# Attention then SwiGLU on one core: PSUM shared out anew, some transposes moved from TensorE to DMA, and the last stores halved

## The chip, the cores and the metric

The kernel runs on one core of a Trainium2 chip. The metric is the device time in microseconds, lower is better. Each kernel was run several times, but for one that got a single look; all runs quoted are of the fast state, but for that one, whose state is unknown. The profile is that of one such run (472.68 us for the kernel before, a run apart from those whose times are listed). "Span" is the time of the profiled execution on the core, about 2 us less than the device time of the same run (470.8 against 472.68 us).

The profile shows five engines: TensorE (PE in the profile, its weight loads PEld), VectorE (DVE), ScalarE (ACT), GpSimd (POOL) and the issuing SyncE (SP). What each waited for is what the profile infers from semaphore events. The kernel puts the results of matmuls in PSUM. A "bank" here is a buffer of up to 512 float32 a partition; the kernel's pools take eight, and in the trace VectorE and ScalarE empty them (a sum's two VectorE instructions take 177 and 424 ns, ScalarE's copy of an output product 491 ns). "Sums" are the products attn @ v of one head, "FFN" is the part after the RMS norm, and a "turn" is a transpose of a whole tile.

## The reference, cut to what matters

```python
# q, k, v: (8, 12, 448, 64)
scores = scale * q @ k^T;  m = max(scores);  e = exp(scores - m)
attn = e / (sum(e) + exp(-m) + 1e-9);  x = attn @ v          # -> (3584, 768)
xn = x / rms(x) * rms_g                                       # RMS norm
out = (silu(xn @ w_gate) * (xn @ w_val)) @ w_out              # 768 -> 1536 -> 768
```

## The kernel before

TensorE executes one hand-ordered stream. After the first batch, the FFN of batch b is woven with the attention of the batches after it: a list `ffn` of units (A: one gate or value product of six matmuls; B: one output product of twelve) gives the beat, and a list `ops` of everything else, each with a time in units, is popped when the beat reaches it. This fixes the *program order* on each engine.

In this kernel q, k and the normalised x have to be turned (transposed) before the matmuls that read them. Some are turned on TensorE into PSUM and copied out, the others by DMA:

```python
    NPE = 2          # batches whose x is turned on TensorE (0 and 1)
    NQPE = 7         # groups of four heads whose q, k are loaded as bf16; 0 to 6 are turned on TensorE
    ps_s = ...tile_pool(name="ps_s", bufs=2, space=PSUM)   # scores: 2 x 2 banks
    ps_u = ...tile_pool(name="ps_u", bufs=2, space=PSUM)   # sums (attn @ v), q/k turns, x turns
    ps_f = ...tile_pool(name="ps_f", bufs=2, space=PSUM)   # FFN products

    def emit_T(g):                                  # q/k turn of one head pair: 16 transposes, one copy
        ps = ps_u.tile([128, 2, C, P], BF16, name="qkt_ps", tag="u")
        ...                                         # nc.tensor.transpose x16
        nc.vector.tensor_copy(out=t[:, :, 0:S], in_=...)          # -> pair_t

    def emit_AV(g, hh):                             # sums of one head: 16 matmuls, emptied by VectorE
        u_ps = ps_u.tile([128, C, E1], FP32, name="u_ps", tag="u")
        ...
        nc.vector.reciprocal(out=recip, in_=u_ps[0:P, :, D:E1])
        nc.vector.tensor_tensor(out=x_tiles[b][...], in0=u_ps[...], in1=recip..., op=ALU.mult)

    def emit_turn_x(b, c):
        if b < NPE:
            ps = ps_u.tile([128, KD, P], BF16, name="xnt_ps", tag="u")
            ...                                     # 6 transposes, one copy
        else:
            nc.sync.dma_start_transpose(out=xnt[:, c, :, :], in_=xn[:, c, :])

    def load_w_o(i):                                # a third of w_out, float32 -> bf16, GpSimd's queue
        nc.gpsimd.dma_start(out=wo_bf[:, i * 4:(i + 1) * 4, :], in_=moe_w_out[i * 512:(i + 1) * 512, :]...)
    ...
    for i in range(KF // 4):
        ops.append((22.1 + 0.01 * i, lambda i=i: load_w_o(i)))
```

`g` counts pairs of heads (six to a batch, NP = 6). Line numbers such as L309 in the profiles are those of the kernel profiled: L309 in the kernel before and L312 in the changed one are the gate and value matmuls, L235 and L238 the sums.

The softmax here doesn't subtract the row's maximum and nothing guards it: scores larger than these inputs give would overflow.

## Time and profile before

475.25 us, median of the three runs (473.12 to 475.77).

From the profile's page, busy time by engine, and the span in 40 slices (busy tenths of TensorE, granted TensorE clock in tenths, busy share of the 16 DMA engines):

```profile
PE 456.7 (97%) x4048; PEld 246.7 (52%) x4048; DVE 241.1 (51%) x621; ACT 249.1 (53%) x365; POOL 95.8 (20%) x109
...
PE   7989998999999999999999989999999999999996
...
PEclk9999999999999999999999999999999999999999
DMA  8999974998099894693069796289015221100133
```

TensorE is the bound: busy 97% of the span, at full clock. What TensorE waited for, from the view of its waits (engine, line, what was waited for: us in total, times, longest):

```profile
PE v_ps L309 <- DVE ht_sb L320: 2.4, 6, 0.6
...
PE u_ps L235 <- DVE pair_t_102 L181: 0.6, 1, 0.6
```

The first is value products waiting for one of the two FFN banks.

### The profile page before, as it was taken

Reading aid. Unit: us, or ns where it says so; the run is one execution under the profiler, and the core shown is the slowest. Engines: PE = TensorE matmul, PEld = TensorE weight load, DVE = VectorE, ACT = ScalarE, POOL = GpSimd, SP = SyncE. Lnnn points to the kernel's source line nnn. Section 1 sums busy time; section 2 is a strip of 40 time slices with the busy share of each in tenths; the row PEclk is TensorE's granted clock in tenths of the full one; section 3 lists DMA queues with packets and bytes.
Section 4 is the critical chain, followed back from the end, with each engine's and each line's share of the span. In section 5 each row is a group of like instructions: output and inputs, shape, how many; then the busy total and the mean of one; then the engine's idle time right before and its main releaser. Section 6 shows DMA issues by size and latency. Waiting matters only on the chain.

```text
span 470.8 us, 9822 instructions
## 1 busy us (share of the span) xinstructions
PE 456.7 (97%) x4048; PEld 246.7 (52%) x4048; DVE 241.1 (51%) x621; ACT 249.1 (53%) x365; POOL 95.8 (20%) x109
## 2 busy tenths in 40 slices
PE   7989998999999999999999989999999999999996
PEld 3644544555555554544555544545455555555563
DVE  5676699455541276656532166755643247555200
ACT  4977764656555665545456555555556652222221
POOL 8424455123020222131011210313000000000000
PEclk9999999999999999999999999999999999999999
DMA  8999974998099894693069796289015221100133
GB/s 134 225 227 190 209 189 101 233 240 156 1 221 170 225 194 114 121 227 66 0 145 194 198 203 144 52 176 181 4 36 127 69 68 24 36 1 0 36 100 100
DMA packets 86776, 60.47 MB, mean 128 GB/s; under 512 B 50646, under 2 KB 81692, under 8 KB 86732
## 3 DMA queue, kind: packets, MB, share of 16 engines
q1 hardware_dynamic: 73820, 43.60, 42.5%
q0 software_dynamic: 12912, 16.26, 18.6%
q8 instruction: 31, 0.51, 0.5%
q14 instruction: 13, 0.11, 0.1%
HBM read 47.19 MB, written 11.01 MB: 124 GB/s over the span
## 4 chain that ended last, share of the span: by engine, by line
PE 85%; DVE 9%; ACT 4%; issue 1%; POOL 0%; DVEq 0%; ACTq 0%
PE o_ps L334 24%; PE v_ps L309 21%; PE g_ps L309 16%; PE u_ps L235 9%; PE s_ps L205 8%; PE s_ps L309 5%; DVE xsq L261 3%; DVE x_sb L239 1%; ACT p_sb_108 L210 1%; DVE ht_sb L320 1%; PE warm_ps L353 1%; ACT t_sb L313 1%; PE qkt_ps L178 1%; ACT p_sb_114 L210 1%; DVE x_sb L266 1%
## 5 line engine op out<-in xcount | busy, mean ns | idle before, releaser
L309 PE MATMUL v_ps<-xnt_sb,wv_bf 128*128 128x448 bf16 x576 | 125.0, 353 | 2.4 <-DVE ht_sb L320 2.4
L334 PE MATMUL o_ps<-wo_bf,ht_sb 128*128 128x384 bf16 x672 | 116.5, 326 | 0.0
L309 PE MATMUL g_ps<-xnt_sb,wg_bf 128*128 128x448 bf16 x444 | 96.4, 353 | 0.7 <-DVE silu_4291 L315 0.6
L334 PEld LDWEIGHTS <-ht_sb 128*128 128x128 bf16 x672 | 62.6, 98 | 46.2 <-issue 7.8
L309 PEld LDWEIGHTS <-wv_bf 128*128 128x128 bf16 x576 | 52.8, 97 | 54.5 <-issue 10.9
L309 PEld LDWEIGHTS <-wg_bf 128*128 128x128 bf16 x576 | 52.2, 97 | 54.2 <-issue 11.2
L313 ACT ACTIVATE t_sb<-g_ps 128x448 f32<-128x448 f32 x74 | 40.3, 544 | 68.7 <-PE g_ps L309 68.6
L210 ACT ACTIVATE p_sb_108<-s_ps 112x896 bf16<-112x896 f32 x64 | 55.5, 915 | 15.6 <-PE s_ps L205 15.5
L210 ACT ACTIVATE p_sb_114<-s_ps 112x896 bf16<-112x896 f32 x64 | 56.0, 919 | 11.8 <-PE s_ps L205 11.8
L337 ACT ACTIVATE out_sb<-o_ps 128x384 f32<-128x384 f32 x56 | 27.5, 491 | 65.6 <-PE o_ps L334 56.2
L210 ACT ACTIVATE p_sb_111<-s_ps 112x896 bf16<-112x896 f32 x64 | 55.7, 918 | 9.5 <-PE s_ps L205 9.5
L238 DVE RECIPROCAL recip<-u_ps 112x4 f32<-112x4 f32 x96 | 17.0, 177 | 82.7 <-PE u_ps L235 82.7
L239 DVE TENSOR_TENSOR x_sb<-u_ps,recip 112x256 bf16<-112x256 f32 x96 | 40.7, 424 | 3.3
L154 POOL CAST q_bf<-q_f 112x1024 bf16<-112x1024 f32 x17 | 17.7, 1040 | 102.7 <-DMA q_f<-in_q_dram 83.9
L292 POOL TENSOR_TENSOR rinv<-ms,neghalf 112x4 f32<-112x4 f32 x8 | 8.3, 1032 | 146.4 <-DVE ms L286 141.5
L205 PE MATMUL s_ps<-qk_t 64*128 64x448 bf16 x272 | 37.5, 354 | 0.0
L261 DVE CUSTOM_DVE_ANT_0 xsq<-x_sb 112x256 bf16<-112x256 bf16 (+3 forms) x62 | 35.2, 568 | 1.6
L313 ACT ACTIVATE t_sb<-s_ps 128x448 f32<-128x448 f32 x22 | 12.0, 544 | 38.5 <-PE s_ps L309 33.3
L309 PE MATMUL s_ps<-xnt_sb,wg_bf 128*128 128x448 bf16 x132 | 28.6, 352 | 0.0
L235 PEld LDWEIGHTS <-p_sb_114 112*128 112x128 bf16 (+1 forms) x512 | 19.8, 97 | 6.7 <-issue 1.4
L235 PEld LDWEIGHTS <-p_sb_111 112*128 112x128 bf16 (+1 forms) x512 | 20.0, 97 | 5.7 <-issue 1.2
L235 PEld LDWEIGHTS <-p_sb_108 112*128 112x128 bf16 (+1 forms) x512 | 19.3, 98 | 6.8 <-issue 2.8
(278 smaller groups left out, 383.0 us busy)
## 6 DMA issues: line engine op xcount, KB each, us to landing
q_f<-in_q_dram SPq DMA_DIRECT2D x15, 448.0 KB, 5.0
k_f<-in_k_dram SPq DMA_DIRECT2D x15, 448.0 KB, 6.3
v_f<-in_v_dram SPq DMA_DIRECT2D x15, 448.0 KB, 7.4
v_f<-in_v_dram POOLq DMA_DIRECT2D x9, 448.0 KB, 9.1
out_dram<-out_sb SPq DMA_DIRECT2D x8, 336.0 KB, 2.8
wg_bf<-in_moe_w_gate_dram POOLq DMA_DIRECT2D x2, 1152.0 KB, 16.5
wv_bf<-in_moe_w_val_dram POOLq DMA_DIRECT2D x2, 1152.0 KB, 14.3
wo_bf<-in_moe_w_out_dram POOLq DMA_DIRECT2D x3, 768.0 KB, 14.9
```

The lines of the kernel that those rows point to most:

```text
L154: eng.tensor_copy(out=dst, in_=staged[n, i].rearrange("p h c d -> p c h d"))
L205: nc.tensor.matmul(s_ps[:, hh, 0:S], lhsT=k_t[r, k0:k0 + 128], rhs=qs[r], start=True, stop=True)
L210: nc.scalar.activation(out=p_v, in_=s_ps[0:P, :, 0:S], func=AF.Exp, scale=scale)
L235: nc.tensor.matmul(u_ps[:, qc, :], lhsT=p_sb[0:K, q0:q0 + 128], rhs=v_sb[0:K, c, h, :], start=(c == 0), stop=(c == C - 1))
L238: nc.vector.reciprocal(out=recip, in_=u_ps[0:P, :, D:E1])
L239: nc.vector.tensor_tensor(out=x_tiles[b][:, :, h * D:(h + 1) * D], in0=u_ps[0:P, :, 0:D], in1=recip.to_broadcast([P, C, D]), op=ALU.mult)
L261: nc.vector.tensor_tensor_reduce(out=xsq[:, 0:n], in0=x_c, in1=x_c, scale=1.0, scalar=0.0, op0=ALU.mult, op1=ALU.add, accum_out=acc)
L292: nc.gpsimd.tensor_tensor(out=rinv, in0=ms, in1=neghalf, op=ALU.pow)
L309: nc.tensor.matmul(ps[:, 0:S], lhsT=w[:, dk, m * 128:(m + 1) * 128], rhs=xnt_tiles[b][:, :, dk, :], start=(dk == 0), stop=(dk == KD - 1))
L313: nc.scalar.activation(out=t, in_=ps[:, 0:S], func=AF.Tanh, scale=0.5)
L334: nc.tensor.matmul(o_ps[:, 0:HN], lhsT=ht_tiles[b2][:, fk, c * 128:(c + 1) * 128], rhs=wo_bf[:, fk, n * HN:(n + 1) * HN], start=(fk == 0), ...
L337: nc.scalar.activation(out=o_sb[:, n * HN:(n + 1) * HN], in_=o_ps[:, 0:HN], func=AF.Copy, scale=0.5)
```

## The change

Its intent: take 56 transposes off TensorE, give the FFN a third PSUM bank so that TensorE waits less for VectorE, and shorten the tail. The sums are left with one bank. The times in the schedule were set anew, and the loads of the output weights moved from 22.1 to 24.0 units.

```diff
-    NPE = 2
-    NQPE = 7
+    NPE = 1
+    NQPE = 6
-    ps_u = ...(name="ps_u", bufs=2)
-    ps_f = ...(name="ps_f", bufs=2)
+    ps_u = ...(name="ps_u", bufs=1)
+    ps_f = ...(name="ps_f", bufs=3)
 def emit_T(g):
-        ps = ps_u.tile([128, 2, C, P], BF16, name="qkt_ps", tag="u")
+        pool, tag = (ps_f, "f") if g < NP else (ps_u, "u")
+        ps = pool.tile([128, 2, C, P], BF16, name="qkt_ps", tag=tag)
 def emit_AV(g, hh):
-        u_ps = ps_u.tile([128, C, E1], FP32, name="u_ps", tag="u")
+        pool, tag = (ps_f, "f") if g < NP and hh == 1 else (ps_u, "u")
+        u_ps = pool.tile([128, C, E1], FP32, name="u_ps", tag=tag)
 def emit_turn_x(b, c):
-            ps = ps_u.tile([128, KD, P], BF16, name="xnt_ps", tag="u")
+            ps = ps_f.tile([128, KD, P], BF16, name="xnt_ps", tag="f")
 def emit_B(b2, c, n):
-        if n == 1:                                 # store both halves of a row block
+        last = b2 == B // 2 - 1 and c == 6
+        if n == 1 or last:                         # the last block: each half as it is done
+            cols = slice(n * HN, (n + 1) * HN) if last else slice(0, DM)
 ... (schedule of the second batch)
-        ops.append((20.4 + 0.5 * c, lambda c=c: emit_scale(1, c)))
-        ops.append((22.2 + 1.1 * c, lambda c=c: emit_turn_x(1, c)))
+        ops.append((19.7 + 0.45 * c, lambda c=c: (emit_scale(1, c), emit_turn_x(1, c))))
+                 (15.6, lambda: turn_qk(2 * NG)), (16.0, lambda: casts(2 * NG + 1)),
-        ops.append((22.1 + 0.01 * i, lambda i=i: load_w_o(i)))
+        ops.append((24.0 + 0.01 * i, lambda i=i: load_w_o(i)))
 ... (other times and the order of some loads and casts left out)
```

More of the change, by code (lines that the diff above doesn't have):

```diff
@@ L60 @@
     ps_s = ctx.enter_context(tc.tile_pool(name="ps_s", bufs=2, space=bass.MemoryType.PSUM))
-    ps_u = ctx.enter_context(tc.tile_pool(name="ps_u", bufs=2, space=bass.MemoryType.PSUM))
-    ps_f = ctx.enter_context(tc.tile_pool(name="ps_f", bufs=2, space=bass.MemoryType.PSUM))
+    ps_u = ctx.enter_context(tc.tile_pool(name="ps_u", bufs=1, space=bass.MemoryType.PSUM))
+    ps_f = ctx.enter_context(tc.tile_pool(name="ps_f", bufs=3, space=bass.MemoryType.PSUM))
     blank = consts.tile([128, 512], BF16, name="blank")
@@ L255, in emit_stats @@
             acc = ss_tiles[b][:, part, c:c + 1]
-            if part > 0 and b < NPE and c % 2 == 1:
+            if part > 0 and b < 2 and c % 2 == 1:
                 xsq2 = tmp.tile([P, 4 * D], BF16, name="xsq2", bufs=1)
@@ L344, in emit_B @@
                 r0 = col - c * 128
-                nc.sync.dma_start(out=out_v[2 * b2 + seg // C, seg % C, p0:p0 + take, :],
-                                  in_=o_sb[r0:r0 + take, :])
+                nc.sync.dma_start(out=out_v[2 * b2 + seg // C, seg % C, p0:p0 + take, cols],
+                                  in_=o_sb[r0:r0 + take, cols])
                 col += take
@@ L365, in ahead @@
         n += AHEAD
-        if NPE * NG + NG <= n < B * NG:
+        if 3 * NG <= n < B * NG:
             if jj == 0:
@@ L386, in micro_ops @@
         b, j = divmod(g, NP)
-        fresh = j == 0 and b <= NPE
+        fresh = j == 0 and b <= 2
         flush = j == NP - 1 and b in (1, B - 1)
@@ L411, in fourth @@
                     finish(b - 1)
-            if b >= NPE:
+            if b >= 2:
                 ahead(*divmod(g, PG))
@@ L436 @@
         ops += [(t0 + (t1 - t0) * i / len(seq), op) for i, op in enumerate(seq)]
-    for j, t0 in enumerate((0.0, 2.3, 4.9, 7.5, 11.6, 14.2, 18.4, 22.5)):
+    for j, t0 in enumerate((0.0, 2.3, 4.9, 7.5, 11.5, 13.9)):
         ops.append((t0, lambda j=j: emit_T(NP + j)))
-    for j, t0 in enumerate((2.2, 4.8, 7.4, 10.0, 12.7, 15.3)):
-        ops += [(t0 + 0.64 * i, op) for i, op in enumerate(micro_ops(NP + j))]
-    ops.append((19.2, lambda: (emit_stats(1, 1), emit_root(1))))
+    for j, t0 in enumerate((2.2, 4.8, 7.3, 9.8, 12.4, 14.9)):
+        ops += [(t0 + 0.61 * i, op) for i, op in enumerate(micro_ops(NP + j))]
+    ops.append((18.65, lambda: (emit_stats(1, 1), emit_root(1))))
     for c in range(C):
-        ops.append((20.4 + 0.5 * c, lambda c=c: emit_scale(1, c)))
-        ops.append((22.2 + 1.1 * c, lambda c=c: emit_turn_x(1, c)))
+        ops.append((19.7 + 0.45 * c, lambda c=c: (emit_scale(1, c), emit_turn_x(1, c))))
     for i in range(KD):
@@ L460 @@
                                 load_qkv(NG + 2, 2, G), cast_qkv(NG + 1, 2, G), load_w(1))),
-                 (7.6, lambda: loads(2 * NG)),
-                 (14.3, lambda: (cast_qkv(NG + 2, 2, G), loads(2 * NG + 1))),
-                 (16.0, lambda: (cast_qkv(2 * NG, 2, G), casts(2 * NG + 1))),
+                 (7.6, lambda: [load_qkv(2 * NG + 1 - i // 3, i % 3, G) for i in (3, 4, 5, 0, 1)]),
+                 (14.3, lambda: (cast_qkv(NG + 2, 2, G), load_qkv(2 * NG + 1, 2, G),
+                                 casts(2 * NG))),
+                 (15.6, lambda: turn_qk(2 * NG)), (16.0, lambda: casts(2 * NG + 1)),
                  (16.1, lambda: loads(2 * NG + 2)), (18.0, lambda: turn_qk(2 * NG + 1)),
-                 (20.0, lambda: casts(2 * NG + 2)), (22.0, lambda: turn_qk(2 * NG + 2))):
+                 (21.2, lambda: casts(2 * NG + 2)), (23.2, lambda: turn_qk(2 * NG + 2))):
         ops.append((t, f))
     for i in range(KF // 4):
-        ops.append((22.1 + 0.01 * i, lambda i=i: load_w_o(i)))
+        ops.append((24.0 + 0.01 * i, lambda i=i: load_w_o(i)))
     ops.sort(key=lambda o: o[0])
@@ L485, in gains @@
     def gains():
-        r_ps = ps_u.tile([128, KD], FP32, name="r_ps", tag="u")
+        r_ps = ps_f.tile([128, KD], FP32, name="r_ps", tag="f")
         nc.tensor.transpose(r_ps, rms_rows, ident_f)
```

## The prediction

> **What bounds it now.** TensorE: the page's first part has it busy 456.7 of 470.8 us, at full granted clock throughout. The change pays only by what it takes off TensorE's in-order stream: instructions or pauses. By the TensorE timeline the pauses are in three places.
> 1. To 36 us: exp on ScalarE is the limit (10.0 of 10 us busy from 10 to 20 us); turning x of batch 0 has pauses of about 0.6 and 0.5 us.
> 2. The second batch (36 to 84 us): VectorE is busy 9.8 and 9.0 of 10 us between 60 and 80 us; TensorE pauses by 0.46 (67.3 us), 0.70 (72.1), 0.53 (77.1) and 0.39 us (80.2).
> 3. Later: six pauses of 0.2 to 0.7 us, sum 3.1 us (121.5, 222.2, 274.6, 279.8, 331.2, 335.9 us), where a gate or value matmul waits for VectorE to empty one of two FFN banks (waits view: v_ps on ht_sb).
> The tail after the last matmul is 4.6 us.
>
> **What it removes.**
> - 24 transposes of x ([...]2.1 us) and two q/k turns (0.5 us each): 3.1 us of TensorE, plus copies on VectorE (two of 0.62, two of 0.5 us) and ScalarE. Pauses 72.1, 77.1 and 80.2 go with them: 1.6 us.
> - A third FFN bank gives VectorE one more unit (1.14 us) of slack, more than any of the six pauses: 3.0 us, and the 0.46 us at 67.3.
> - x of batch 0 through three banks: 0.5 us. Last stores in halves: 0.3 us.
>
> **What it adds.** With one bank for sums, each use waits for VectorE to empty the one before. From batch 2 on this is free: in the trace the next sum starts 1.4 us or more after the last was emptied, but for the last pair (0.1 us). In the second batch it costs: in the new order of TensorE a sum directly follows a q/k turn on the same bank three times. In the old trace the turn's copy ended 0.8, 1.6 and 2.1 us after the following sum began (the copy is 0.62 us, behind other work in VectorE's queue); smaller overlaps of 0.2 to 0.3 us occur three times. VectorE catches up while TensorE waits, so I estimate 4 us in all. [...]
> DMA: two more q/k turns and four x turns (1.3 us of issue, about 1.6 us more to land, each) between 62 and 84 us, wanted some 8 us later: nothing exposed. GpSimd gets two more casts (1.04 us), off the path.
>
> **Sum.** −3.1 −1.6 −3.5 −0.5 −0.3 + 4 = about −5 us, up to −6, nearly all on the critical path, which is TensorE's stream. From 475.25: 469.6 us, range 466.5 to 473.0. Chances: faster by over 2% 0.08, within 2% 0.90, slower 0.02.
>
> **What would show it.** 56 fewer TensorE matmuls; no wait of v_ps on ht_sb over 0.3 us after 82 us; new waits of u_ps on the q/k copy (pair_t) of about 1 us, three times, between 42 and 66 us; the second batch's stage only 1 to 2 us shorter; x turns landing 3 us or more before their first matmul.
>
> **What would make it wrong.** The single bank costing more than 4 us because VectorE's queue is fuller than I think, which brings the gain near zero; or less, if these waits replace ones it would have had anyway. x turned too late, behind q/k turns in the one DMA issue queue, would stall the FFN of batch 1 by microseconds. The run-to-run spread (473.1 to 475.8) is half the gain.

Two passages are cut from the prediction, at the places marked. The sum came to about −5 us (469.6 us) as recorded, and all its terms stand in it, the +4 us for the single bank among them. One passage is a time for each transpose of x, which the traces don't show. The 2.1 us for the 24 is the author's estimate; the trace before has TensorE busy with them for 1.86 us, 77 ns each. In the trace before the sum at 72.81 us waits 0.57 us for a turn's copy, and the value product behind it starts at 73.31 us.

## More of the kernel before

From TensorE's timeline (start, duration, engine, line, operation, how many; in brackets the idle time before and what ended it), a case of two sums after a q/k turn with two banks for the three, and the place where the FFN of the second batch starts:

```profile
71.57 0.67 PE L235 MATMUL u_ps<-v_sb_120,p_sb_114 113*128 113x65 bf16 x16
72.81 0.67 PE L235 MATMUL u_ps<-v_sb_120,p_sb_114 113*128 113x65 bf16 x16 [0.57 <-DVE pair_t_102 L181]
...
85.27 0.55 PE L205 MATMUL s_ps<-pair_t_104 64*128 64x448 bf16 x4
85.75 1.31 PE L309 MATMUL g_ps<-xnt_sb,wg_bf 128*128 128x448 bf16 x6
```

At 85.75 us the FFN of batch 1 follows its predecessor without a gap. Three stretches, by milestones of the stream: the FFN of batch 0 with the attention of batch 1; the first half of the FFN of batch 1; the rest up to the start of the last matmul (stretch, its length, then busy time and count by engine, clock, DMA share, GB/s):

```profile
35.57:85.75 50.18, 48.31 (x535) 25.31 (x533) 38.76 (x93) 33.20 (x49) 23.88 (x27) 1.00 0.89 175
85.75:104.26 18.51, 18.51 (x171) 9.67 (x169) 9.26 (x23) 11.59 (x16) 3.64 (x4) 1.00 1.16 235
104.26:465.81 361.55, 359.06 (x2940) 194.34 (x2939) 169.60 (x432) 177.51 (x263) 49.40 (x48) 1.00 0.51 111
```

## The result, and the profile after

487.15 us, median of four runs (486.41 to 487.92), against 474.77: slower. The ratio is 1.0264, 95% interval 1.0229 to 1.0300.

From the page after:

```profile
PE 456.8 (94%) x3992; PEld 245.0 (50%) x3992; DVE 238.5 (49%) x618; ACT 248.4 (51%) x363; POOL 97.7 (20%) x111
...
PE   7989977359999999999999999999999999999996
...
PEclk8999999869999999999999999999999999999999
DMA  8999996999408879569309779369304420300133
```

There are 56 matmuls fewer, as planned, yet TensorE's busy time didn't fall, because part of it ran at a lower clock (mean granted clock 0.979, against 1.000 before): the granted clock drops in the first slice and around the eighth and ninth, where TensorE is also busy only 0.3 and 0.5 of the time while the DMA engines are busy. TensorE's waits:

```profile
PE g_ps L312 <- DMA xnt_sb<-x_sb: 13.0, 1, 13.0
PE s_ps L207 <- DVE pair_t_102 L183: 2.0, 1, 2.0
PE u_ps L238 <- DVE pair_t_106 L183: 1.9, 2, 1.2
PE u_ps L238 <- DVE pair_t_104 L183: 1.6, 1, 1.6
PE v_ps L312 <- DVE silu_1454 L318: 1.5, 1, 1.5
PE u_ps L238 <- DVE x_sb L242: 1.3, 3, 0.6
```

One wait of 13.0 us is the news: the first gate product of batch 1 waits for x turned by DMA. The waits on the FFN banks (ht_sb) are gone from the list. The timelines of TensorE, of the DMA issue queue (SPq) and of GpSimd around it:

```profile
83.17 6.77 SPq L285 DMA_TRANSPOSE xnt_sb<-x_sb  x4
90.04 8.02 SPq L167 DMA_TRANSPOSE qk_t<-q_bf  x1
...
85.10 2.42 POOL L125 DMA_DIRECT2D wo_bf<-in_moe_w_out_dram  x3
...
88.92 0.74 PE L207 MATMUL s_ps<-qk_t 64*128 64x448 bf16 x4
102.69 2.42 PE L312 MATMUL g_ps<-xnt_sb,wg_bf 128*128 128x448 bf16 x6 [13.03 <-DMA xnt_sb<-x_sb]
```

The four x turns are issued from 83.17 us on, right after VectorE scaled x. In the middle of that, at 85.10 us, GpSimd issues all three loads of the output weights. By the trace, the first two x turns land 2.6 and 2.7 us after their issue began and the third after 11.4 us. The fourth is on the chain of work that ended last (start, duration, what):

```profile
87.13 15.51 DMA xnt_sb<-x_sb
102.64 0.04 issue
102.69 2.42 PE g_ps L312 x6
```

It took 15.5 us. The gate product after the stop also takes 2.42 us where it took 1.31: the clock. The trace's clock records give half clock from 7.5 to 14.3 us and from 92.8 to 106.5 us.

What the DMA engines moved from 90 to 100 us (queue, packets, MB, and the time that the packets took as a share of 16 engines):

```profile
q0 software_dynamic: 1144, 1.71, 94.4%
q1 hardware_dynamic: 1127, 0.28, 21.7%
```

GpSimd's queue (q0, the output weights) and SyncE's (q1, the turns) pass the same *number* of packets, but 1.71 MB against 0.28. Counted from the packet records, in stretches of 2 us (92:94 and 96:98, which look like their neighbours, left out):

```
us        1536-byte packets (output weights)   256-byte packets (turns)
84:86        0                                    893
86:88       44                                    451
88:90      231                                      9
90:92      213                                    197
94:96      226                                    217
98:100     227                                    224
100:102    149                                    614
102:104      0                                   1418
```

One x turn is 112 x 768 bf16 = 672 packets of 256 bytes. Two of them (1344) have passed by 87 us; then only 9 packets in 3 us, and then one for one with the weights until these end just after 101 us.

The stretches after, with the same milestones:

```profile
37.25:102.69 65.44, 46.04 (x477) 23.25 (x477) 37.77 (x91) 32.70 (x47) 26.12 (x29) 0.92 0.95 175
102.69:122.99 20.30, 20.30 (x168) 10.45 (x169) 9.03 (x22) 10.75 (x15) 6.27 (x6) 0.91 0.97 213
122.99:481.20 358.21, 358.21 (x2941) 193.90 (x2939) 168.35 (x432) 177.53 (x263) 46.69 (x45) 1.00 0.49 108
```

Subtracting those of before splits the 14.7 us by which the span grew (470.8 to 485.5):

| Stretch | before, us | after, us | difference |
|---|---|---|---|
| to the first FFN matmul | 35.57 | 37.25 | +1.7 (half clock from 7.5 us; see below) |
| FFN of batch 0 with the attention of batch 1 | 50.18 | 65.44 | +15.3, of which 13.0 the wait on x |
| first half of the FFN of batch 1 | 18.51 | 20.30 | +1.8 (half clock to 106.5 us) |
| from there to the start of the last matmul | 361.55 | 358.21 | −3.3 (third FFN bank) |
| tail, from the start of the last matmul | 4.98 | 4.32 | −0.7 (stores in halves) |

### The profile page after: what moved, and what is told of

Its sections match the earlier page's. It is cut to its first block, busy times and chain, and to the rows that moved or that the text cites. A ratio compares the mean times of both kernels' runs of the same rounds, so it can differ in the third digit from the quotient of the medians.

```text
span 485.5 us, 9743 instructions
## 1 busy us (share of the span) xinstructions
PE 456.8 (94%) x3992; PEld 245.0 (50%) x3992; DVE 238.5 (49%) x618; ACT 248.4 (51%) x363; POOL 97.7 (20%) x111
## 4 chain that ended last, share of the span: by engine, by line
PE 79%; DMA 9%; issue 6%; POOL 5%; DVE 1%; ACT 0%; POOLq 0%
PE o_ps L337 23%; PE v_ps L312 20%; PE g_ps L312 15%; PE u_ps L238 8%; PE s_ps L207 7%; PE s_ps L312 5%; DMA xnt_sb<-x_sb 3%; DMA q_f<-in_q_dram 2%; DMA qk_t<-q_bf 2%; DMA v_f<-in_v_dram 1%; POOL v_f L143 1%; POOL v_sb_117 L154 1%; POOL k_bf L143 1%; POOL q_bf L143 1%; DVE x_sb L269 0%
## 5 line engine op out<-in xcount | busy, mean ns | idle before, releaser
L312 PE MATMUL g_ps<-xnt_sb,wg_bf 128*128 128x448 bf16 x444 | 97.5, 356 | 13.2 <-DMA xnt_sb<-x_sb 13.0
L154 POOL CAST q_bf<-q_f 112x1024 bf16<-112x1024 f32 x18 | 18.7, 1040 | 124.4 <-DMA q_f<-in_q_dram 99.9
L207 PE MATMUL s_ps<-qk_t 64*128 64x448 bf16 x288 | 39.9, 354 | 0.0
## 6 DMA issues: line engine op xcount, KB each, us to landing
wg_bf<-in_moe_w_gate_dram POOLq DMA_DIRECT2D x2, 1152.0 KB, 14.3
```

Of the source, the lines that this page charges most:

```text
L154: eng.tensor_copy(out=dst, in_=staged[n, i].rearrange("p h c d -> p c h d"))
L207: nc.tensor.matmul(s_ps[:, hh, 0:S], lhsT=k_t[r, k0:k0 + 128], rhs=qs[r], start=True, stop=True)
L312: nc.tensor.matmul(ps[:, 0:S], lhsT=w[:, dk, m * 128:(m + 1) * 128], rhs=xnt_tiles[b][:, :, dk, :], start=(dk == 0), stop=(dk == KD - 1))
```

## The experiments

Theory A: the stop is the last x turns sharing the DMA engines packet for packet with the output weights, which GpSimd issues as soon as its own queue lets it; the half clock after it follows from the stop. Rival B: x comes late because of the order on the one DMA issue queue, behind the q/k turns. Rival C: the new bank split is what made the kernel slow. Twelve kernels were run; all gave correct results. "Before" is the kernel before on the same chip.

### The output weights loaded later

```diff
 # changed kernel, one line
-        ops.append((24.0 + 0.01 * i, lambda i=i: load_w_o(i)))
+        ops.append((31.0 + 0.01 * i, lambda i=i: load_w_o(i)))
```

On GpSimd's queue the loads then stand behind casts that wait for a later load of q and k; in the trace they are issued at 100.5 us instead of 85.1.

> The changed kernel with only the three loads of the output weights moved behind the casts of group 9 on GpSimd's queue, so that they can't run while x of the second batch is being turned by DMA. Theory A (the 13.0 us stop of TensorE at 89.6 us is the last x turns sharing the DMA engines packet for packet with these loads, and the half clock from 92.8 to 106.5 us follows from the stop): all four x turns land within about 4 us of their issue, no TensorE wait on x over 1 us, no clock drop there; 487.2 less 13.4 less 1.8 = about 472 us. Rival B (x comes late because of the order on the DMA issue queue, q/k turns first): the stop stays and the time stays near 487 us.

Measured: 472.50 us (before 473.54; ratio 0.9970, interval 0.9943 to 0.9997). The wait on x is gone from TensorE's waits, whose longest are now:

```profile
PE u_ps L238 <- DVE pair_t L183: 3.5, 3, 1.6
PE s_ps L207 <- DVE pair_t L183: 1.9, 2, 1.6
PE u_ps L238 <- DVE x_sb L242: 1.6, 3, 0.8
PE v_ps L312 <- DVE silu L318: 1.5, 1, 1.5
```

The first three x turns land 2.6 to 2.7 us after their issue began, and the clock records are full from 15.3 us to the end of the work. From 84 to 90 us the DMA engines pass 2828 packets, nearly all of 256 bytes (the rest are of 4), 471 per us with the gaps between turns included, against 113 per us beside the weights (1127 in 10 us):

```profile
q1 hardware_dynamic: 2828, 0.69, 60.2%
```

14.65 us came back between the medians (14.3 between the two profiled spans, both with an early half clock of 6.8 us), against 13.0 + 1.8 read from the trace. The order on the issue queue is the same in both, the x turns before the q/k turns, so B falls.

### A third of the cost

The first of the three loads at 24.0 as in the change, the other two at 31.0.

> The changed kernel with the first of the three output-weight loads where the change has it and the other two behind the casts of group 9: a third of the suspected cost. In the changed kernel's trace about 113 packets of the weights' load and 113 of the x turns passed per us in turn. One load is about 512 packets, so 4.5 us of sharing, in which about 512 x packets pass; the rest then pass at the free rate. Theory A (sharing packet for packet): TensorE's wait on x shrinks from 13.0 to about 2 to 3 us. If the last x turn were late for a cause of its own (issue order, GpSimd, the turn itself), it would stay near 13 us or go to 0 as with all loads moved.

Measured, one look, state unknown: 480.60 us (span 478.6, clock records at half from 93.5 to 100.3 us).

```profile
PE g_ps L312 <- DMA xnt_sb<-x_sb: 4.9, 1, 4.9
```

13.0, 4.9 and 0 us for three loads, one and none: the stop follows the weights. I had 2 to 3 us; the packet records show why it is more. In the 2 us after the load started (88 to 90 us) no packet of a turn passed, before the taking of turns began. I had counted only the sharing. Why they stand still at first is open. The load's own packets are few there too: 71 from 88 to 89 us, where 131 pass in the next.

### x by DMA alone, in the kernel before

```diff
 # kernel before
-        if b < NPE:
+        if b < 1:
             ps = ps_u.tile([128, KD, P], BF16, name="xnt_ps", tag="u")
```

> The kernel before with one thing changed: x of the second batch is turned by DMA, not TensorE; PSUM, q/k of group 6, and the output weights' loads as before (these are issued by GpSimd at about 80 us, just as x turns would be issued). Theory A: the same stop of TensorE, 10 to 15 us, before the FFN of the second batch, with a clock drop after it; about 475 - 3 + 13 + 2 = 487 us. Rival (the stop needs the other parts, such as the extra q/k turn): no stop, 471 to 473 us.

Measured: 494.04 us (before 473.54; ratio 1.0425, interval 1.0398 to 1.0452). The weights are issued at 82.0 us and the x turns from 82.44 us on, so they meet. Half clock from 92.4 to 109.5 us.

```profile
PE g_ps L309 <- DMA xnt_sb<-x_sb: 17.3, 1, 17.3
```

The stop needs neither the new banks nor the extra q/k turn. It is what one asks for by turning x by DMA at the time of that load. I expected 487 us; both the stop and the stretch of half clock were longer. The trace shows why for the stop: in this schedule loads of q, k and v stand before the fourth x turn in SyncE's queue. The first three turns, held up beside the weights, took 9.1 us to issue, so the fourth was issued only at 96.4 us; its packets then stood behind those loads and it landed after 8.6 us. Here the order on the issue queue, which rival B names, adds to what the weights cost; how much each gives was not separated.

### The banks back at two and two, in the changed kernel

```diff
-    ps_u = ...bufs=1      ps_f = ...bufs=3
+    ps_u = ...bufs=2      ps_f = ...bufs=2
```

> The changed kernel with two banks for sums and two for the FFN again, all else as changed. If the single bank for sums costs 3 us in the second batch's stage (as the trace of the changed kernel says between 37 and 79 us) and the third FFN bank gives 3 us after 120 us, the time stays near 487 us and the two parts show in the milestones: the second batch's attention about 3 us shorter, the rest about 3 us longer. If the bank split were the main cause of the slowdown, the time would fall by 5 us or more.

Measured: 486.66 us (ratio to before 1.0276, interval 1.0236 to 1.0316), the changed kernel's time. From the first FFN matmul to the start of the nineteenth FFN unit, where the attention of batch 1 ends, it takes 39.0 us against the changed kernel's 42.0, and from the milestone at 123 us to the last matmul 360.9 against 358.2: both as expected. The stop on x is 9.8 us, a little shorter, but the turns took no less: from the issue of the first x turn to the gate product it is 19.5 us in both kernels (78.64 to 98.09, and 83.17 to 102.69 us). TensorE only came to its wait later, 9.7 us after that issue against 6.5. The six waits on FFN banks are back.

```profile
PE g_ps L312 <- DMA xnt_sb<-x_sb: 9.8, 1, 9.8
PE v_ps L312 <- DVE ht_sb L323: 3.3, 6, 1.1
```

So C falls as the cause of the slowdown.

### The banks alone, in the kernel before

The pools and tags as in the change; x and q/k turned as before.

> The kernel before with only the PSUM shared out anew (one bank for sums, three for the FFN, x turned through the FFN banks). Third bank: the six waits on the FFN banks after 82 us go, -3 us; single bank for sums with three to four q/k turns directly before a sum: +3 to +4 us in the second batch's stage. Sum: 474 to 476 us, the same as before. If the bank split were what made the changed kernel slow: 480 us or more.

Measured: 479.70 us (ratio 1.0120, interval 1.0094 to 1.0146). I expected no change, and had named 480 us as the sign that the split is the cause; two of the four runs lie over it (480.20 and 480.25). So this kernel alone does not clear C: the split costs some 6 us under the old schedule. It is the pair of changed kernels above, 487.15 and 486.66 us (ratios 1.0264 and 1.0276), that clears it.

```profile
PE u_ps L237 <- DVE pair_t L182: 5.9, 4, 2.8
```

The stretch of batch 1's attention took 59.5 us instead of 50.2; the rest, from its end to the last matmul, gained 3.3 us. Within a wait of 2.8 us from 65.7 us the clock falls to half, from 67.6 to 74.4 us: here the fall of the clock began during a wait on one bank. The old schedule has two more q/k turns on the single bank, and waits 5.9 us for them against 3.5; that this is why it fares worse is tested next.

### The same with the q/k turns in the FFN's banks

```diff
 # banks alone, in the kernel before, and
 def emit_T(g):
-        pool, tag = (ps_f, "f") if g < NP else (ps_u, "u")
+        pool, tag = ps_f, "f"
```

> The kernel before with the new PSUM shares, but every q/k turn through the FFN banks, so no sum follows a turn on the single bank. If the loss of the bank split alone (479.7 us against 473.5) is the turns sharing the sums' bank, this gives back 6 us and keeps the third FFN bank's 3 us: 470 to 472 us. If one bank for sums is too few in itself, it stays at 477 us or more.

Measured: 474.15 us (ratio 0.9989, interval 0.9958 to 1.0021): 5.5 us of the 6 came back between the medians (all of it by the ratios, 1.0120 to 0.9989), so the turns sharing the sums' bank were most of the loss. But it is the same as before, not faster: the attention of batch 1 still takes 53.2 us instead of 50.2 (sums wait 1.5 us for the single bank, a gate product 1.8 us for an FFN bank that a turn now shares), which eats the third bank's gain later.

### Control: the later load in the kernel before

> Control: the kernel before with its output-weight loads moved behind the casts of group 9, nothing else. If the move itself gives time in any kernel, this one gets faster; I expect the same as before within 0.3 per cent (473 to 475 us), as no x is turned by DMA there and the weights are wanted only at 124 us.

Measured: 475.35 us (before 474.57; ratio 1.0015, interval 0.9984 to 1.0046). The move gives nothing where x isn't turned by DMA.

### The turns alone, with the load out of their way

The later load, and PSUM two and two.

> The changed kernel with late output-weight loads and PSUM two and two: what turning x and q/k by DMA is worth by itself (with the last stores in halves). No wait on x, none of u_ps on a turn's copy, but the six waits for FFN banks are back. By the sum: 474 less 3.1 (transposes), less 1.6 (pauses that went with them), less 0.65 (tail) = about 469 us; if those pauses only move to other places, 471 us.

Measured: 474.59 us (472.45 to 477.07; ratio 1.0002, interval 0.9965 to 1.0040). I expected 469 to 471. The stretch of batch 1's attention, first the kernel before's line as shown above (50.18 us long, TensorE busy 48.31), here:

```profile
36.66:86.36 49.70, 46.17 (x477) 23.44 (x477) 36.55 (x91) 32.21 (x47) 24.14 (x26) 1.00 0.93 181
```

TensorE is busy 2.1 us less, but the stretch is only 0.5 us shorter: its idle time rose from 1.9 to 3.5 us. The pauses that I had booked as gone did go, and others took their place:

```profile
PE v_ps L312 <- DVE ht_sb L323: 2.8, 6, 0.6
PE s_ps L207 <- DVE pair_t L183: 2.5, 3, 1.3
PE g_ps L312 <- DVE silu L318: 1.6, 2, 1.4
```

All three are waits on VectorE. Inside the stretch they are 1.6 us (silu), 1.0 us (pair_t) and 0.7 us (ht_sb), against five waits of 0.2 to 0.6 us, 1.8 in all, in the kernel before. The runs spread by 4.6 us, three of the four at the same granted clock of 0.996; I have no explanation for that spread.

### The q/k turns in the FFN's banks, in the changed kernel

The later load, and `emit_T` as in the edit above.

> The changed kernel with late output-weight loads, and the q/k turns of the second batch in the FFN's banks, so that no sum waits for a turn's copy on the single bank. The waits of u_ps on the turns' copies (3.5 us in three) go, and so does part of the 1.6 us of waits of u_ps on x; the FFN units may wait a little more for a bank. Against 472.5 us: 468 to 470 us. If TensorE's waits there only stand in for VectorE being late anyway, no gain: 472 us.

Measured: 469.52 us (469.05 to 471.65; ratio 0.9910, interval 0.9867 to 0.9952). No sum waits for a turn's copy any more; 3 us less than with the later load alone, in line with the 3.5 us of waits.

### The start filled

```diff
     emit_T(0)
+    warm(8)
```

> The changed kernel with late output-weight loads, and 8 warm-up matmuls more after the first q/k turn, to fill TensorE's 2 us wait at 5.3 us. If the half clock from 8 to 15 us in some runs of every kernel (granted clock 0.991 to 0.993, against 0.999, in the runs of the kernel before too, 1.6 us apart) comes from that idle time, all runs keep 0.998 or more and the median falls by about 1 us, to 471.5 us, with less spread.

Measured: 471.24 us (470.85 to 471.49; ratio 0.9932, interval 0.9903 to 0.9961); all four runs at a granted clock of 1.0. In the same call the kernel before had three runs at 0.999 or 1.0 (472.93 to 473.05 us), two at 0.992 (475.09 and 475.71), and two at 0.995 and 0.998 (474.57 and 475.08). A mean clock lower by 0.007 over 473 us is 6.6 us at half clock, the length of the early stretch in the traces that have one (7.5 to 14.3 us in the changed kernel's, 8.0 to 14.8 us in the control's). So that stretch isn't a part of the change: by run, it befalls the kernel before too (read from mean clocks; its own profiled run has none), and costs some 2 us, though the last of those seven runs shows that not all of the spread is clock. With the wait of TensorE after the first turn filled, these four runs had none. The kernel before was not run with the same filling, so part of this gain is not the change's.

### Versions meant to beat both

First the later load, q/k turns in the FFN's banks, and the filled start together:

> Late output-weight loads, q/k turns in the FFN banks, and the start filled with 8 more warm-up matmuls. The parts add: 469.0 to 469.5 us in every run, granted clock 0.998 or more, against 469.5 with runs up to 471.7 without the filling.

Measured: 469.73 us, six runs from 469.30 to 470.91 (ratio 0.9902, interval 0.9878 to 0.9925). No better than without the filling; three runs still had a clock of 0.996, so the filling isn't a full cure.

Then one set of four banks for sums, turns and FFN, with the later load and the filled start:

```diff
-    ps_u = ...bufs=1
-    ps_f = ...bufs=3
+    ps_f = ...bufs=4          # every ps_u.tile(..., tag="u") is now ps_f.tile(..., tag="f")
```

> As the one before (late output-weight loads, start filled), but sums, q/k turns and the FFN take turns in one set of four banks. The remaining waits of sums for VectorE to empty the single bank (2.3 us in three) go, as a buffer comes round only after three others; the FFN units then have between two and three banks. 467 to 469 us if no new waits on FFN banks come; 470 us or more if they do.

Measured, as expected: 467.84 us, five runs from 467.15 to 468.39 (before 475.12; ratio 0.9857, interval 0.9830 to 0.9885). This is the fastest of all, 1.4% under the kernel before. No wait of a sum on a bank is left; what is left:

```profile
PE g_ps L311 <- DMA xnt_sb<-x_sb: 1.8, 1, 1.8
PE s_ps L206 <- DVE pair_t L182: 1.2, 2, 1.0
...
PE g_ps L311 <- DVE silu L317: 1.0, 1, 1.0
```

The first line says that the x turns have no time to spare here even with the weights out of the way.

## Why the prediction was wrong

The prediction was 469.6 us (466.5 to 473.0), with 0.02 for slower by over 2%. Point by point:

- **"Wanted some 8 us later: nothing exposed." This is the step that failed, twice over.** I had looked at the DMA share before (0.75 from 60 to 70 us and 0.44 from 70 to 80; the same view has 1.04 from 80 to 90), as if the load there would stay where it was. But x turned on TensorE had never met the 768 KB loads that GpSimd issues at about 80 us; x turned by DMA does. The output weights stood *after* the x turns in the schedule's list, but that list orders only within an engine, and GpSimd wasn't held back by anything: it went from a cast begun at 83.99 us straight to the loads at 85.10. Cost: 13.0 us of wait and 1.8 us of half clock after it; moving the load gave back 14.65. And the spare time was not 8 us: the scaling of x ends at 85.7 us, the first matmul that needs all of it could have started at 89.7 us, and the fourth turn, issued at 87.1 us behind the other three, would have landed at 89.8 us even at the clean 2.7 us. In the run with the later load, the fourth turn was issued at 87.5 us and the gate product went at 90.1 us, with no wait on x but no margin either. The prediction named late x turns as a risk, but for another reason (issue order), which in the changed kernel was not it: there the x turns are issued before the q/k turns.
- **The third FFN bank, −3.0 us after the second batch: right.** The waits on ht_sb are gone and the stretch to the last matmul is 3.3 us shorter.
- **The single bank for sums, +4 us: right in mechanism and nearly in size.** The changed kernel's sums wait 3.5 us for turns' copies (1.9 + 1.6), in three places, and 1.3 us for other sums. Between the two runs with and without it (both with the later load) the stretch is 52.85 against 49.70 us, 3.2 us.
- **The transposes, −3.1 us, and three pauses, −1.6 us: mis-sized.** By themselves they shortened the stretch by 0.5 us, not 4.7. Busy time fell by 2.1 to 2.3 us; the pauses came back in other places, all as waits on VectorE. That its queue, and not the transposes, made the old ones too is how I read this; no run tests it. I had listed "these waits replace ones it would have had anyway" for the new waits, and not asked it of the old ones that I took away.
- **Batch 0's x through three banks, −0.5 us: not seen.** Among profiled runs without the early half clock the first FFN matmul starts at 35.57 us in the kernel before, and with the change's banks at 35.69 (changed kernel, start filled) and 35.61 us (banks alone); only with all q/k turns in the FFN's banks, or one set of four, is it at 35.26 to 35.35. **The last stores, −0.3 us:** 0.66 us.
- **The run-to-run spread** was read as noise. Much of it goes with the granted clock (472.93 to 473.05 us at 0.999 or 1.0, 475.09 and 475.71 at 0.992), and the traces that show where put it in the first 15 us: by luck of the run, up to about 2 us.

Without the stop the change was worth about 1 us (472.50 against 473.54, the interval of the ratio ending at 0.9997), not 5; with the start filled besides, 3 us (471.24 against 474.57).

In the changed kernel's trace the two queues pass a packet each in turn: 1144 and 1127 in 10 us. With 1536 bytes to a packet of the weights and 256 to one of the turns, the turns got 0.28 of 1.99 MB, a seventh. And the trace before, which I had, shows it already. From 83 to 87 us the same weights ran beside loads of q, k and v on SyncE's queue:

```profile
q0 software_dynamic: 368, 0.57, 77.4%
q1 hardware_dynamic: 367, 0.38, 34.3%
```

The load of v issued at 81.5 us, behind those of q and k and beside the weights, landed after 17.3 us, where the median of the 15 such loads is 7.4. With this a stop could have been foreseen. My estimate afterwards, with the measured 113 per us: the four turns' 2688 packets, all beside the weights, are 24 us, less what passes before and after the load. In the changed kernel, where two of the four had passed before it, 19.5 us went by from the first issue to the gate product.

The clock fell 3.1 us after the stop began (89.7 to 92.8 us) and stayed at half for 13.7 us. In the banks alone it fell 1.9 us into a wait of 2.8 us, and stayed for 6.8 us; the early half clocks follow waits of 1.3 to 2.0 us, and the same kernel has them in some runs and not in others (mean clocks of the kernel before from 0.992 to 1.0). What brings it on, and after how long a wait, these runs do not show.

## What to carry to other kernels

Before work is moved from an engine to DMA, list what else is queued on the DMA engines *at the moment it will run*, by packets and not by bytes: here an urgent stream of small packets beside a load of large ones ran four times slower (113 packets per us against 471), and the schedule's order held nothing back across queues, as no wait did. Putting the load behind something that runs late on its own queue was enough. One shared set of four banks beat the fixed split of one and three (467.84 against 469.73 us), and a pause that seems to belong to an instruction may belong to the engine that is behind, and come back when the instruction is gone (here 2.1 us less of TensorE work shortened the stretch by 0.5 us).

## What else the traces show

- A DMA transpose beside a bulk load: x turns passed 113 packets per us beside 1536-byte packets, against 471 per us by themselves, and landed after 11.4 and 15.5 us instead of 2.7.
- There were 3 us in which almost no packet of the turns passed (9 of them from 87 to 90 us) after the load started; the load's own packets were few at first too (32 from 87 to 88 us, 107 in the next). The cause is open.
- Four x turns with a q/k turn after them, alone on the DMA engines (the later load), moved 115 GB/s on average from 84 to 90 us, gaps included, with single slices up to 239. Turns of this size (172 KB) are issued 1.2 to 1.3 us apart, which alone allows about 138 GB/s by my estimate from these two numbers. Where turns had piled up behind the load and then ran alone (102.5 to 103.3 us in the changed kernel) they moved 284 GB/s.
- The early half clock costs about 2 us of 475, as much as the gains being measured; a comparison needs the granted clock of each run beside its time.
